# Attention feeding a maxout feed-forward layer on one Trainium2 core: the first batch's odd-token queries ahead of its even-token queries, with loads and transposes of the opening reordered

## The chip, the core and the metric

The kernel runs on one core of a Trainium2 chip. Its time is the device time of one execution in microseconds, as the median of several runs. Lower is better. The profile is that of one execution.

## The reference

The reference has two stages. Attention has 8 batches, 12 heads, 448 tokens and a head size of 64; its softmax adds exp(-max) to the denominator, so that the weights of a row may sum to less than one. The 3584 x 768 result goes through three 768 x 768 products, the largest of the three is kept for each element, and a fourth 768 x 768 product follows.

```python
def _attn_ref(q, k, v):
    scale = 1.0 / np.sqrt(q.shape[-1])
    scores = scale * np.matmul(q, k.transpose(0, 1, 3, 2))
    m = np.max(scores, axis=-1, keepdims=True)
    e = np.exp(scores - m)
    attn = e / (np.sum(e, axis=-1, keepdims=True) + np.exp(-m) + 1e-09)
    return np.matmul(attn, v).astype(np.float32)

def _moe_ref(x, w1, w2, w3, w_out):
    h = np.maximum(np.maximum(x @ w1, x @ w2), x @ w3)
    return (h @ w_out).astype(np.float32)
```

Since e / (sum e + exp(-m)) equals exp(s) / (sum exp(s) + 1) where s is the scaled score, the kernel takes exp(s) directly and needs no maximum.

## The kernel before

**Units of work.** The 12 heads of a batch are three groups of four heads, so there are 24 groups; group 0, 1 and 2 are batch 0, and group 3 begins batch 1. A group has two pairs of heads. One group's q, k and v are loaded by DMAs that GpSimd (POOL in the profile) issues in program order, with a cast from 32 to 16 bits: `load_qk` (L101, DMA at L113) and `load_v` (L118, two DMAs). `load_weight` (L133, L137) loads one of the four weights in three DMAs of two 128-row blocks each. Each of `ld_q`, `ld_k`, `ld_v` has four buffers, so group 4 uses the buffers of group 0.

**Attention of a group.** q and k must be transposed. `transpose_pe` (L182) transposes one pair's k and q blocks on TensorE into a PSUM tile `trT`, and copies them out into `KT` and `QT` with `evac`, on ScalarE (ACT) or VectorE (DVE). `transpose_once` (L217) transposes all of q or k, and then `shift_q` (L241) makes the shifted copy on POOL. `scores` (L285) multiplies 64-row blocks of k by the queries into PSUM tiles `stp`, and one exponential on ACT (L319) writes them to the buffer `e`. `av_tail` and `av_main` (L329, L348) multiply the exponentials by v, and DVE divides (L366 to L372) into `xn`. `prep_v` (L379) first copies v into the layout that they read, on DVE or POOL. `x_transpose_pe` (L392) transposes the result into `xT`, the input of the feed-forward layer.

**Feed-forward pieces.** `up_piece` (L430) makes two of six 128-row blocks of one of the three products for a range of batch 0's tokens, as 12 matmuls with 256 or 192 columns, in the order of the weights: w0 for the three pairs of blocks, then w1, then w2. DVE keeps the running maximum in `hT`. `out_piece` makes the last product. Pieces stand in a list, and `fill(cols)` takes pieces from it for as long as a credit of columns lasts, so that TensorE's program order mixes attention and pieces.

**Even and odd tokens.** In batch 0 the queries of each group are done in two parts: "E" is 256 of the 448 queries, "O" the other 192, selected by `part_blocks`. An opening loop does six steps: E of groups 0, 1, 2, and then O of groups 0, 1, 2. The loop over groups 3 to 23 follows, in three visits for each group. Step n computes scores of its own part and the product with v for the part before it. The first piece is made in step 3, and a piece of 256 columns goes with each half of steps 4 and 5 and with visits 0 and 1 of group 3. Visit 0 of group 3 also transposes q of group 4.

**The order on each engine is the program's.** The kernel runs under a manual schedule, so what is written first goes first on its engine. The pool `ps_s` has three PSUM tiles for scores, products with v and some transposes; `ps_b` has two, for the other transposes and the pieces.

**POOL's order before the change**: q of group 0, k of group 0 in two halves, the identity, q and k of group 1, v of 0, q and k of 2, v of 1, v of 2; then w0, `prep_v(1)`, q and k of 3, `prep_v(2)`, w1, w2, v of 3, k and q of 4, `shift_q(3)`, v of 4, k and q of 5, w_out. `prep_v(0)` is done by DVE.

Of the kernel before, what the change touches and what calls it, by code (L numbers as in the profile page):

```python
# [14 lines left out]
ts = bass.ts  # L15
# [6 lines left out]
def kernel(  # L22
# [78 lines left out]
    def load_qk(i, names="kq", prs=(0, NP)):  # L101
        b, g = groups[i]
        tiles = raw.setdefault(i, {})
        for nm in names:
            if nm not in tiles:
                t = ld_bufs[nm][i % NL]
                if nm == "q" and i < NF:
                    nc.vector.memset(t[:, 0 : NP * T + 2 : NP * T + 1, :], 0.0)
                tiles[nm] = t
            src = {"q": q, "k": k}[nm][b].rearrange("h s d -> (h s) d")  # L110
            src = src.rearrange("(g r x t) d -> g x r (t d)", g=NG, r=NP, x=P)[g]
            p0, p1 = prs
            nc.gpsimd.dma_start(  # L113
                out=tiles[nm][:, 1 : NP * T + 1].rearrange("x (r t) d -> x r (t d)", r=NP)[:, p0:p1],
                in_=src[:, p0:p1],
            )
# [16 lines left out]
    def load_weight(i, gs=(0, 1, 2)):  # L133
        w = (moe_w1, moe_w2, moe_w3, moe_w_out)[i]
        src = w.rearrange("(g hf p) f -> g p hf f", g=3, hf=2)
        for g in gs:
            nc.gpsimd.dma_start(out=w_sb[i][:, 2 * g : 2 * g + 2, :], in_=src[g])  # L137
# [1 line left out]

    wz = cpool.tile([128, 512], MMDT, name="wz")  # L140
    nc.vector.memset(wz, 0.0)
    load_qk(0, "q")
    load_qk(0, "k", (0, 1))
    load_qk(0, "k", (1, 2))
    ident16 = cpool.tile([128, 128], MMDT, name="ident16")
    make_identity(nc, ident16)
    load_qk(1)
# [10 lines left out]
        nc.vector.memset(vt_buf[j][:, :, D : D + 2], 1.0 / LAMBDA)  # L158
    for j in range(NEB):
        nc.vector.memset(e_buf[j][:, NB * S : NB * S + HP], 0.0)  # L160

    def warm(n, cols=512):
        ps = ps_b.tile([128, 512], FP32, tag="b", name="warm")
        for _ in range(n):
            nc.tensor.matmul(  # L165
                out=ps[:, 0:cols], lhsT=wz[:, 0:128], rhs=wz[:, 0:cols], start=True, stop=True
            )
# [8 lines left out]
    def evac(eng, dst, src):  # L176
        if eng is nc.scalar:
            nc.scalar.activation(out=dst, in_=src, func=AF.Copy)  # L178
        else:
            eng.tensor_copy(out=dst, in_=src)  # L180

    def transpose_pe(i, pr, pool, k_eng, q_engs):  # L182

        if pool is ps_s:
            both = ps_s.tile([128, 2, 1024], MMDT, tag="s", name="trT")
            tps = [both[:, 0], both[:, 1]]
        else:
            tps = [ps_b.tile([128, 1024], MMDT, tag="b", name="trT") for _ in range(2)]
        kr, qr = raw[i]["k"], raw[i]["q"]
        def tr(n, j, src, t):  # L190
            nc.tensor.transpose(  # L191
                out=tps[n][:, ts(j, 128)],
                in_=src[:, t + 1 : t + 3, :].rearrange("x t d -> x (t d)"),
                identity=ident16,
            )

        kj = (0, 1, 2) if pr == 0 else (3, 4, 5, 6)
        qt = (-1, 1, 3, 5, 0, 2, 4, 6) if pr == 0 else (8, 10, 12, 7, 9, 11, 13)
        for j, b in enumerate(kj):
            tr(0, j, kr, 2 * b)  # L200
        for j, t in enumerate(qt):
            tr(1, j, qr, t)
# [3 lines left out]
        evac(  # L206
            k_eng,
            KT[i][:, kj[0] * 128 : (kj[-1] + 1) * 128],
            tps[0][:, 0 : len(kj) * 128],
        )  # L210
        q0 = pr * 1024
        n = -(-len(qt) // len(q_engs))
        for e, eng in enumerate(q_engs):
            a, b = e * n * 128, min((e + 1) * n, len(qt)) * 128
            evac(eng, QT[i][:, q0 + a : q0 + b], tps[1][:, a:b])

    def transpose_once(i, nm, eng):  # L217

# [291 lines left out]
    def fill(cols):  # L510
        credit[0] += cols
        while pieces and credit[0] > 0:
            f, a, w = pieces.pop(0)
            f(*a)
            credit[0] -= w
        if not pieces:
            credit[0] = min(credit[0], 0.0)
# [2 lines left out]
        return sum(w for _, _, w in pieces)  # L520


    DV, AC = nc.vector, nc.scalar
    warm(10)
    transpose_pe(0, 0, ps_s, DV, (AC, DV))
    warm(3)
    transpose_pe(0, 1, ps_b, DV, (DV,))
    load_weight(0)
    prep_v(1, nc.gpsimd)
    load_qk(3)  # L530
    prep_v(2, nc.gpsimd)
    load_weight(1)

    parts = [(part, g) for part in "EO" for g in range(NG)]
    PW = {"E": (0, 1), "O": (2, 3), "EO": (0, 1, 2, 3)}
    UPE = 2 * NDC * (NE + 6)

    def av(i, ej, pr, part):
        av_tail(i, ej, pr, PW[part])
        av_main(i, ej, pr, PW[part])  # L540

    for n, (part, g) in enumerate(parts):
        ej = n % NEB
        pp, pg = parts[n - 1] if n > 0 else (None, None)
        step = UPE if n > 3 else 0
        nxt = g + 1 if part == "E" and g < NG - 1 else None
        scores(g, ej, (0, 1), part)
        if n != 3:
            scores(g, ej, (2, 3), part)
        if n > 0:  # L550
            av(pg, 1 - ej, 0, pp)
        if n > 1 and n != 4:
            x_transpose_pe(parts[n - 2][1], parts[n - 2][0])
        if n == 3:
            av(pg, 1 - ej, 1, pp)
            scores(g, ej, (2, 3), part)
        if n == 4:
            transpose_once(3, "q", AC)
        fill(step)
        if nxt is not None and n > 0:  # L560
            transpose_pe(nxt, 0, ps_b, AC, (DV,))
        scores(g, ej, (4, 5), part)
        scores(g, ej, (6,), part)
        if n == 0:
            warm(4)
            transpose_pe(nxt, 0, ps_b, DV, (DV,))
            prep_v(0, DV)
        if n == 3:
            x_transpose_pe(pg, pp)
            add_up(0, 0, NE, [(i, f) for i in range(3) for f in (0, 2, 4)])  # L570
            fill(UPE)
        if nxt is not None:
            transpose_pe(nxt, 1, ps_b, DV, (AC, DV) if n == 0 else (DV,))
        if n > 0 and n != 3:
            av(pg, 1 - ej, 1, pp)
        if n == 4:
            transpose_once(3, "k", AC)
        fill(step)
        if n == 1:
            load_weight(2)  # L580
        if n == 2:
            load_v(3)
            load_qk(4)
        if n == 4:
            shift_q(3, nc.gpsimd)
            load_v(4)
            load_qk(5)
            load_weight(3)


    visits = ((0, 1), (2, 3), (4, 5, 6))
# [18 lines left out]
    for i in range(3, NI):  # L610
        ej, pj = (i + 1) % NEB, i % NEB
        first = i == 3
        if PE_QK <= i + 2 < NI:
            transpose_dma(i + 2)
        if first:
            load_v(i + 2)
        for vi, units in enumerate(visits):
            n = 3 * i + vi
            scores(i, ej, units)
            if i == 4 and vi == 0:  # L620
                prep_v(i, DV)
            if vi < 2:
                av(i - 1, pj, vi, "O" if first else "EO")
            if vi == 1 and i > 3 * PE_X:
                x_transpose_dma(i - 1)
            if n in adds:
                add_batch(adds[n])
            per = UPE if first and vi < 2 else share(n)
            if vi == 0 and first:
                x_transpose_pe(1, "O")  # L630
            if vi == 2 and first:
                x_transpose_pe(i - 1, "O")
                fill(per / 2)
                prep_v(i, DV)
                add_up(0, NE, NO, [(w, f) for w in range(3) for f in (0, 2, 4)])
                add_out(0)
                per = share(n)
            if vi == 2 and 3 < i <= 3 * PE_X:
                x_transpose_all(i - 1)
            if first and vi == 1:  # L640
                transpose_once(i + 1, "q", AC)
                fill(per)
# [54 lines left out]
```

## Time and profile before

| | |
|---|---|
| median of 6 runs | 344.98 us |
| lowest, highest | 343.57, 346.86 us |
| profiled execution, its own time | 346.86 us |
| span of its instructions | 345.1 us |
| mean granted TensorE clock | 0.994 |
| TensorE (PE) busy | 331.7 us, 96% |
| VectorE (DVE), ScalarE (ACT), GpSimd (POOL) busy | 187.4, 151.7, 147.3 us |
| bytes moved by DMA, mean rate | 46.20 MB, 134 GB/s |

The profiled execution is the slowest of the six, and its own time is 1.8 us longer than its span. In the profile's lines, the first number of a timeline row is the start in us from the start of the span, the second how long it took, then engine, source line, operation, tile written and tiles read, shape and count; in square brackets is the idle time of the engine ahead of it and what ended it. Rates count bytes as written in 16 bits. A row with several shapes or instructions covers them all from the first start to the last end.

### The profile page before, as it was taken

The numbers are of one execution on the slowest core, as the hardware profiler recorded it, in microseconds if no ns is written. First come the engines' busy times: TensorE is split into PE (matmuls) and PEld (weight loads), VectorE is DVE, ScalarE is ACT, GpSimd is POOL, SyncE is SP. The second block draws the span as 40 slices with busy tenths as digits, with TensorE's granted clock in tenths as the row PEclk, the third lists the DMA queues.
The fourth block names the chain that finished last, engine by engine and source line by source line (L and its number), as shares of the span: only waits on it lengthen the run. The fifth ranks groups of instructions, "written<-read, shape, count | busy, mean of one in ns | idle before, by whom it ended". The sixth has DMA issues, their size and how long they took to land.

```text
span 345.1 us, 9827 instructions
## 1 busy us (share of the span) xinstructions
PE 331.7 (96%) x4184; PEld 200.6 (58%) x4184; DVE 187.4 (54%) x407; ACT 151.7 (44%) x181; POOL 147.3 (43%) x262
## 2 busy tenths in 40 slices
PE   8889699999999999999999999999999999999993
PEld 4668478866556555556555655556556555555552
DVE  2655357555556556556556555555556556465552
ACT  2876456566454444443443443453544444200000
POOL 8685558594683364272566075173354000000000
PEclk9999899999999999999999999999999999999999
DMA  7999999789897997979997999979982440133015
GB/s 103 187 208 209 201 163 159 111 132 216 147 140 119 200 218 106 123 113 238 144 125 105 189 195 123 110 126 220 135 145 10 122 123 3 33 76 93 0 41 144
DMA packets 84797, 46.20 MB, mean 134 GB/s; under 512 B 53264, under 2 KB 81296, under 8 KB 84752
## 3 DMA queue, kind: packets, MB, share of 16 engines
q0 software_dynamic: 29392, 22.03, 48.5%
q1 hardware_dynamic: 55120, 23.37, 38.0%
q8 instruction: 33, 0.54, 0.6%
q10 hardware_dynamic: 240, 0.16, 0.2%
q14 instruction: 12, 0.10, 0.1%
HBM read 44.04 MB, written 11.01 MB: 160 GB/s over the span
## 4 chain that ended last, share of the span: by engine, by line
PE 89%; ACT 4%; DMA 3%; DVE 1%; issue 1%; ACTq 0%
PE p_i L439 46%; PE op_ps L463 16%; PE stp L299 11%; PE avp L356 10%; DMA ld_q<-in_q_dram 3%; ACT e L319 3%; PE avp L339 2%; PE warm L165 2%; ACT QT L178 1%; PE trT L191 1%; PE trT L224 1%; PE xtp L412 0%; DVE QT L180 0%; DVE xn L372 0%; DVE xT L405 0%
## 5 line engine op out<-in xcount | busy, mean ns | idle before, releaser
L319 ACT ACTIVATE e<-stp 128x896 f16<-128x896 f32 (+4 forms) x171 | 144.1, 904 | 136.3 <-PE stp L299 136.3
L439 PE MATMUL p_i<-xT,w 128*128 128x448 f16 (+2 forms) x972 | 174.7, 333 | 0.3
L439 PEld LDWEIGHTS <-w 128*128 128x128 f16 x972 | 90.5, 98 | 68.0 <-issue 5.0
L244 POOL COPY QT<-QT 64x384 f16<-64x384 f16 (+1 forms) x84 | 46.7, 556 | 101.6 <-DMA QT<-ld_q 82.1
L450 DVE TENSOR_TENSOR hT<-hT,p_i 128x448 f16<-128x448 f16 (+2 forms) x96 | 59.6, 621 | 48.6 <-PE p_i L439 48.5
L463 PE MATMUL op_ps<-w,hT 128*128 128x384 f16 (+2 forms) x342 | 58.3, 323 | 0.0
L299 PE MATMUL stp<-QT,KT 64*64 64x448 f16 (+2 forms) x756 | 47.6, 338 | 1.7 <-DVE xn L372 0.7
L463 PEld LDWEIGHTS <-hT 128*128 128x128 f16 x342 | 32.1, 98 | 22.9 <-issue 2.0
L356 PE MATMUL avp<-vx,e 128*128 128x65 f16 x1152 | 45.4, 193 | 0.0
L470 DVE TENSOR_SCALAR o_sb<-op_ps 128x384 f32<-128x384 f32 (+2 forms) x57 | 31.3, 550 | 23.7 <-PE op_ps L463 22.8
L448 DVE CAST hT<-p_i 128x448 f16<-128x448 f32 (+2 forms) x48 | 30.0, 624 | 24.3 <-PE p_i L439 24.2
L356 PEld LDWEIGHTS <-e 128*128 128x128 f16 x1152 | 38.8, 97 | 2.2
L372 DVE TENSOR_TENSOR xn<-avp,rb 128x512 f16<-128x512 f32 (+1 forms) x54 | 34.1, 632 | 2.1 <-DVE rb L369 0.2
L299 PEld LDWEIGHTS <-KT 64*64 64x64 f16 x756 | 15.6, 105 | 26.3 <-issue 21.8
L366 DVE TENSOR_SCALAR rb<-avp 128x8 f32<-128x8 f32 (+1 forms) x54 | 8.9, 166 | 39.5 <-PE avp L356 39.4
L382 POOL COPY vx<-ld_v 128x768 f16<-128x768 f16 x21 | 17.2, 819 | 6.3 <-issue 3.7
L339 PEld LDWEIGHTS <-e 64*64 64x64 f16 x768 | 14.7, 107 | 7.8 <-PE stp L299 0.7
L113 POOL DMA_DIRECT2D ld_q<-in_q_dram x24 | 17.7, 740 | 3.2 <-PE stp L299 1.2
L113 POOL DMA_DIRECT2D ld_k<-in_k_dram x25 | 17.9, 718 | 2.5 <-PE avp L356 1.5
L126 POOL DMA_DIRECT2D ld_v<-in_v_dram x24 | 15.2, 634 | 2.1 <-DMA ld_q<-in_q_dram 1.1
L339 PE MATMUL avp<-vt,e 64*64 64x65 f16 x768 | 15.4, 192 | 0.6 <-DVE xn L372 0.5
L123 POOL DMA_DIRECT2D ld_v<-in_v_dram x24 | 15.2, 633 | 1.1 <-DMA ld_k<-in_k_dram 0.6
(40 smaller groups left out, 91.2 us busy)
## 6 DMA issues: line engine op xcount, KB each, us to landing
out_dram<-o_sb SPq DMA_DIRECT2D x54, 192.0 KB, 3.7
ld_v<-in_v_dram POOLq DMA_DIRECT2D x48, 128.0 KB, 4.9
ld_q<-in_q_dram POOLq DMA_DIRECT2D x24, 224.0 KB, 7.1
ld_k<-in_k_dram POOLq DMA_DIRECT2D x23, 224.0 KB, 6.7
w<-in_moe_w_dram POOLq DMA_DIRECT2D x9, 384.0 KB, 9.2
w<-in_moe_w_out_dram POOLq DMA_DIRECT2D x3, 384.0 KB, 9.3
xT<-xn SPq DMA_TRANSPOSE x18, 4.6
QT<-ld_q SPq DMA_TRANSPOSE x17, 5.9
```

The source lines that it names most:

```text
L113: nc.gpsimd.dma_start(out=tiles[nm][:, 1 : NP * T + 1].rearrange("x (r t) d -> x r (t d)", r=NP)[:, p0:p1], in_=src[:, p0:p1],)
L244: eng.tensor_copy(out=t[d0 : d0 + HP, o * 128 : (o + n) * 128], in_=t[s0 : s0 + HP, a * 128 : (a + n) * 128],)
L299: nc.tensor.matmul(out=stp[half * HP : half * HP + HP, par, j * qn : (j + 1) * qn], lhsT=k_block(i, pr, h2, x[half]), rhs=q_cols(i, pr, h2 ...
L319: nc.scalar.activation(out=dst, in_=src, func=AF.Exp, scale=scale)
L339: nc.tensor.matmul(out=ps[half * HP : half * HP + HP, hh, j * D1 : (j + 1) * D1], lhsT=eF[hh * HP : hh * HP + HP, o : o + HP], rhs=vt[hh * ...
L356: nc.tensor.matmul(out=ps[:, hh, j * D1 : (j + 1) * D1], lhsT=eF[:, o : o + 128], rhs=vx[:, 2 * pr + hh, (x[0]), 0:D1], start=False, stop= ...
L372: nc.vector.tensor_tensor(out=xn[i][:, pr, ws[0] : ws[0] + nw].rearrange("p j h d -> p h j d"), in0=acc[:, :, :, 0:D], in1=rb[:, :, 0:nw]. ...
L439: nc.tensor.matmul(out=p_i[:, j * qn : (j + 1) * qn], lhsT=w_sb[i][:, dc, ts(fc, 128)], rhs=xT[b][:, dc, q0 : q0 + qn], start=(dc == 0), s ...
L448: nc.vector.tensor_copy(out=dst, in_=src)
L450: nc.vector.tensor_tensor(out=dst, in0=dst, in1=src, op=ALU.max)
L463: nc.tensor.matmul(out=op_ps[:, 0:w], lhsT=hT[bp][:, fc, ts(t, 128)], rhs=wout_sb[:, fc, c : c + w], start=(fc == 0), stop=(fc == NFC - 1),)
L470: nc.vector.tensor_scalar(out=o_sb[:, c : c + w], in0=op_ps[:, 0:w], scalar1=1.0 / LAMBDA, scalar2=None, op0=ALU.mult,)
```

## The change

It has five parts.

1. Batch 0's order is turned: O (192 queries) of groups 0, 1, 2 first, then E (256 queries). The pieces for the O tokens are made first, 192 columns wide, two of them in step 3; the E pieces come after them. `STEP` takes the place of `UPE` as the credit. Since E is no longer written first, the columns of `e` between the parts are set to zero by a memset for each buffer.
2. In steps 0 to 2, scores of units 0 and 1 (which need the first pair only) come ahead of the second pair's transposes; before, all transposes of a group came ahead of its scores, or in the step before.
3. `transpose_pe` gives each job (k, and each part of q) a PSUM tile of its own in place of one shared tile or of one for k and one for q.
4. Group 0's k and q are loaded as k and q of pair 0, then k and q of pair 1.
5. POOL's order after v of 2 becomes: `prep_v(0)` (moved here from DVE), two thirds of w0, `prep_v(1)`, the last third of w0, q and k of 3, `prep_v(2)`, w1, **k and q of 4, w2, v of 3**, `shift_q(3)`, v of 4, k and q of 5, w_out.

```diff
-    load_qk(0, "q")
-    load_qk(0, "k", (0, 1))
-    load_qk(0, "k", (1, 2))
+    load_qk(0, "kq", (0, 1))
+    load_qk(0, "kq", (1, 2))
...
         nc.vector.memset(e_buf[j][:, NB * S : NB * S + HP], 0.0)
+        blk = e_buf[j][:, 0 : NB * S].rearrange("p (n s) -> p n s", s=2 * S)
+        nc.vector.memset(blk[:, :, NO : NO + HP], 0.0)
...
     def transpose_pe(i, pr, pool, k_eng, q_engs):
-        if pool is ps_s:
-            both = ps_s.tile([128, 2, 1024], MMDT, tag="s", name="trT")
-            tps = [both[:, 0], both[:, 1]]
-        else:
-            tps = [ps_b.tile([128, 1024], MMDT, tag="b", name="trT") for _ in range(2)]
+        def tile_of():
+            if pool is ps_s:
+                return ps_s.tile([128, 2, 1024], MMDT, tag="s", name="trT")[:, 0]
+            return ps_b.tile([128, 1024], MMDT, tag="b", name="trT")
...
+        n = -(-len(qt) // len(q_engs))
+        jobs = [(k_eng, "k", kj[0], kr, [2 * b for b in kj])]
+        for e, eng in enumerate(q_engs):
+            jobs.append((eng, "q", pr * 8 + e * n, qr, qt[e * n : (e + 1) * n]))
+        tps = [tile_of() for _ in jobs]
...
-    warm(3)
-    transpose_pe(0, 1, ps_b, DV, (DV,))
-    load_weight(0)
-    prep_v(1, nc.gpsimd)
+    prep_v(0, PL)
+    load_weight(0, (0, 1))
+    prep_v(1, PL)
+    load_weight(0, (2,))
     load_qk(3)
-    prep_v(2, nc.gpsimd)
+    prep_v(2, PL)
     load_weight(1)
-    parts = [(part, g) for part in "EO" for g in range(NG)]
-    UPE = 2 * NDC * (NE + 6)
+    STEP = 2 * NDC * (NO + 6)
+    parts = [(part, g) for part in "OE" for g in range(NG)]
     for n, (part, g) in enumerate(parts):
         scores(g, ej, (0, 1), part)
+        if n < 3:
+            if n == 0:
+                warm(2)
+            transpose_pe(g, 1, ps_b, DV, (DV,))
             scores(g, ej, (2, 3), part)
+            if n > 0:
+                av(pg, 1 - ej, 0, pp)
+            if n == 1:
+                transpose_pe(2, 0, ps_b, AC, (DV,))
+            if n == 2:
+                x_transpose_pe(0, "O")
+            scores(g, ej, (4, 5), part)
+            scores(g, ej, (6,), part)
+            if n > 0:
+                av(pg, 1 - ej, 1, pp)
+            else:
+                warm(4)
+                transpose_pe(1, 0, ps_b, AC, (DV,))
+                load_qk(4)
+                load_weight(2)
+                load_v(3)
+        elif n == 3:
             av(pg, 1 - ej, 0, pp)
+            x_transpose_pe(1, "O")
             av(pg, 1 - ej, 1, pp)
             scores(g, ej, (2, 3), part)
+            x_transpose_pe(2, "O")
+            add_up(0, NE, NO, [(i, f) for i in range(3) for f in (0, 2, 4)])
+            fill(STEP)
+            scores(g, ej, (4, 5), part)
+            scores(g, ej, (6,), part)
+            fill(STEP)
+        else:
+            scores(g, ej, (2, 3), part)
+            av(pg, 1 - ej, 0, pp)
+            if n == 4:
+                transpose_once(3, "q", AC)
+            else:
+                x_transpose_pe(0, "E")
+            fill(STEP)
+            scores(g, ej, (4, 5), part)
+            scores(g, ej, (6,), part)
             av(pg, 1 - ej, 1, pp)
+            if n == 4:
+                transpose_once(3, "k", AC)
+            fill(STEP)
+            if n == 4:
+                shift_q(3, PL)
+                load_v(4)
+                load_qk(5)
+                load_weight(3)
...
-                av(i - 1, pj, vi, "O" if first else "EO")
+                av(i - 1, pj, vi, "E" if first else "EO")
...
             if vi == 2 and first:
-                x_transpose_pe(i - 1, "O")
+                x_transpose_pe(i - 1, "E")
                 fill(per / 2)
                 prep_v(i, DV)
-                add_up(0, NE, NO, [(w, f) for w in range(3) for f in (0, 2, 4)])
+                add_up(0, 0, NE, [(w, f) for w in range(3) for f in (0, 2, 4)])
                 add_out(0)
```

Before, the loads of w2 stood at the end of step 1, and those of v of 3 and q and k of 4 at the end of step 2.

More of the change, by code (lines that the diff above doesn't have):

```diff
@@ L182, in transpose_pe @@
     def transpose_pe(i, pr, pool, k_eng, q_engs):
-        if pool is ps_s:
-            both = ps_s.tile([128, 2, 1024], MMDT, tag="s", name="trT")
-            tps = [both[:, 0], both[:, 1]]
-        else:
-            tps = [ps_b.tile([128, 1024], MMDT, tag="b", name="trT") for _ in range(2)]
-        kr, qr = raw[i]["k"], raw[i]["q"]
[L190 to L195, printed above, removed]
+        def tile_of():
+            if pool is ps_s:
+                return ps_s.tile([128, 2, 1024], MMDT, tag="s", name="trT")[:, 0]
+            return ps_b.tile([128, 1024], MMDT, tag="b", name="trT")
+        kr, qr = raw[i]["k"], raw[i]["q"]
         kj = (0, 1, 2) if pr == 0 else (3, 4, 5, 6)
         qt = (-1, 1, 3, 5, 0, 2, 4, 6) if pr == 0 else (8, 10, 12, 7, 9, 11, 13)
[L199 to L202, printed above, removed]
+        n = -(-len(qt) // len(q_engs))
+        jobs = [(k_eng, "k", kj[0], kr, [2 * b for b in kj])]
+        for e, eng in enumerate(q_engs):
+            jobs.append((eng, "q", pr * 8 + e * n, qr, qt[e * n : (e + 1) * n]))
         if i not in KT:
@@ L205, in transpose_pe @@
             QT[i] = att_pool.tile([P, (NB + 1) * 128], MMDT, tag="QT", name="QT")
[L206 to L215, printed above, removed]
+        tps = [tile_of() for _ in jobs]
+        for tp, (eng, nm, o, src, toks) in zip(tps, jobs):
+            for j, t in enumerate(toks):
+                nc.tensor.transpose(
+                    out=tp[:, ts(j, 128)],
+                    in_=src[:, t + 1 : t + 3, :].rearrange("x t d -> x (t d)"),
+                    identity=ident16,
+                )
+        for tp, (eng, nm, o, src, toks) in zip(tps, jobs):
+            dst = {"k": KT, "q": QT}[nm][i]
+            evac(eng, dst[:, o * 128 : (o + len(toks)) * 128], tp[:, 0 : len(toks) * 128])
     def transpose_once(i, nm, eng):
@@ L520, in left @@
         return sum(w for _, _, w in pieces)
-    DV, AC = nc.vector, nc.scalar
-    warm(10)
-    transpose_pe(0, 0, ps_s, DV, (AC, DV))
-    warm(3)
-    transpose_pe(0, 1, ps_b, DV, (DV,))
-    load_weight(0)
-    prep_v(1, nc.gpsimd)
-    load_qk(3)
-    prep_v(2, nc.gpsimd)
-    load_weight(1)
-    parts = [(part, g) for part in "EO" for g in range(NG)]
+    DV, AC, PL = nc.vector, nc.scalar, nc.gpsimd
     PW = {"E": (0, 1), "O": (2, 3), "EO": (0, 1, 2, 3)}
-    UPE = 2 * NDC * (NE + 6)
+    STEP = 2 * NDC * (NO + 6)
     def av(i, ej, pr, part):
@@ L540, in av @@
         av_main(i, ej, pr, PW[part])
+    warm(10)
+    transpose_pe(0, 0, ps_s, DV, (AC, DV))
+    prep_v(0, PL)
+    load_weight(0, (0, 1))
+    prep_v(1, PL)
+    load_weight(0, (2,))
+    load_qk(3)
+    prep_v(2, PL)
+    load_weight(1)
+    parts = [(part, g) for part in "OE" for g in range(NG)]
     for n, (part, g) in enumerate(parts):
@@ L544 @@
         pp, pg = parts[n - 1] if n > 0 else (None, None)
-        step = UPE if n > 3 else 0
-        nxt = g + 1 if part == "E" and g < NG - 1 else None
         scores(g, ej, (0, 1), part)
-        if n != 3:
+        if n < 3:
+            if n == 0:
+                warm(2)
+            transpose_pe(g, 1, ps_b, DV, (DV,))
             scores(g, ej, (2, 3), part)
-        if n > 0:
+            if n > 0:
[15 more added lines that the diff above has]
+        elif n == 3:
@@ L551 @@
             av(pg, 1 - ej, 0, pp)
-        if n > 1 and n != 4:
-            x_transpose_pe(parts[n - 2][1], parts[n - 2][0])
-        if n == 3:
+            x_transpose_pe(1, "O")
             av(pg, 1 - ej, 1, pp)
             scores(g, ej, (2, 3), part)
[L557 to L574, printed above, removed]
-            av(pg, 1 - ej, 1, pp)
-        if n == 4:
-            transpose_once(3, "k", AC)
@@ L578 @@
[L578 to L588, printed above, removed]
+            x_transpose_pe(2, "O")
[14 more added lines that the diff above has]
+            scores(g, ej, (6,), part)
+            av(pg, 1 - ej, 1, pp)
+            if n == 4:
[6 more added lines that the diff above has]
+                load_weight(3)
@@ L627 @@
                 add_batch(adds[n])
-            per = UPE if first and vi < 2 else share(n)
+            per = STEP if first and vi < 2 else share(n)
             if vi == 0 and first:
-                x_transpose_pe(1, "O")
+                x_transpose_pe(1, "E")
             if vi == 2 and first:
-                x_transpose_pe(i - 1, "O")
+                x_transpose_pe(i - 1, "E")
                 fill(per / 2)
                 prep_v(i, DV)
-                add_up(0, NE, NO, [(w, f) for w in range(3) for f in (0, 2, 4)])
+                add_up(0, 0, NE, [(w, f) for w in range(3) for f in (0, 2, 4)])
                 add_out(0)
```

## The prediction

> **What bounds the kernel now.** I read the engine shares first, then PE's waits in two stretches, then the order of time around the one long wait, then the loads behind it.
>
> ```profile
> PE 331.7 (96%) x4184; PEld 200.6 (58%) x4184; DVE 187.4 (54%) x407; ACT 151.7 (44%) x181; POOL 147.3 (43%) x262
> ```
>
> PE is the engine to look at. Its waits up to 44 us, and then from 44 us to the end:
>
> ```profile
> PE trT L224 <- DMA ld_q<-in_q_dram: 3.1, 1, 3.1
> PE warm L165 <- DVE wz L141: 1.2, 1, 1.2
> PE stp L299 <- DVE xn L372: 0.7, 1, 0.7
> PE avp L339 <- DVE xn L372: 0.5, 1, 0.5
> ```
>
> ```profile
> PE trT L224 <- ACT QT L178: 0.3, 1, 0.3
> ```
>
> After 44 us PE waits 0.3 us in 300. So whatever PE gains ahead of that point reaches the end one for one, and the opening decides. PE's order of time there:
>
> ```profile
> 36.35 0.57 PE L299 MATMUL stp<-QT,KT 64*64 64x448 f16 x8
> ...
> 37.31 0.38 PE L399 MATMUL xtp<-ident,xn 128*128 128x128 f16 x4
> 40.85 0.93 PE L224 MATMUL trT<-ident,ld_q 128*128 128x128 f16 x7 [3.15 <-DMA ld_q<-in_q_dram]
> 41.57 2.62 PE L439 MATMUL p_i<-xT,w 128*128 128x256 f16 x12
> 44.12 0.57 PE L299 MATMUL stp<-QT,KT 64*64 64x448 f16 x8
> ```
>
> In visit 0 of group 3, PE stops at 37.69 for q of group 4. When it goes on, a piece of 12 matmuls takes 2.62 us where others take 1.40 (from one start to the next, 27.58 to 28.98). The stretches of the wait, behind it and after that show why (columns: PE, PEld, DVE, ACT, POOL busy, then granted clock, DMA share, GB/s):
>
> ```profile
> 37.70:40.40 2.70, 0.00 (x0) 0.00 (x0) 0.87 (x3) 0.88 (x2) 2.20 (x4) 1.00 1.34 198
> 40.50:43.90 3.40, 3.05 (x18) 2.34 (x19) 0.00 (x0) 0.92 (x1) 1.51 (x3) 0.50 1.23 206
> 43.90:47.00 3.10, 3.04 (x50) 2.33 (x48) 1.48 (x5) 2.39 (x3) 0.00 (x0) 1.00 1.16 212
> ```
>
> The clock was halved for 3.4 us behind the gap: 7 transposes and a piece took 3.27 us (40.85 to 44.12), not 0.39 + 1.40 = 1.79. So the wait cost 3.15 + 1.5 us. The DMA engines were full meanwhile (198 GB/s), so the load was late by its place in the queue. POOL's order:
>
> ```profile
> 19.79 4.19 POOL L137 DMA_DIRECT2D w<-in_moe_w_dram  x6
> 24.58 0.62 POOL L123 DMA_DIRECT2D ld_v<-in_v_dram  x1 [0.60 <-DMA ld_k<-in_k_dram]
> 25.40 0.61 POOL L126 DMA_DIRECT2D ld_v<-in_v_dram  x1 [0.20 <-issue]
> 27.53 0.70 POOL L113 DMA_DIRECT2D ld_k<-in_k_dram  x1 [1.51 <-PE avp L356]
> 29.43 0.70 POOL L113 DMA_DIRECT2D ld_q<-in_q_dram  x1 [1.20 <-PE stp L299]
> ```
>
> The tile's own answers give the times to landing: 10.3 us for w1's last DMA (issued 21.2, landed 31.5), 13.9 us for w2's last (23.2, 37.2), 11.4 us for q of group 4 (29.4, 40.8). One after another at one rate: w2's three DMAs of 384 KB take 31.5 to 37.2, 1.9 us each or 202 KB/us; v of 3, k and q of 4 (704 KB) take 3.6 us. Both waits of POOL at the two loads end as an older DMA lands (w1's first two land at 27.0 and 28.9), whatever engine the brackets name.
>
> **Part 1: the order of loads.** k and q of 4 (448 KB) go ahead of w2 and v of 3. At 202 KB/us that is 2.2 us: q of 4 lands at 31.5 + 2.2 = 33.7 instead of 40.8, and the last of w2 at 37.2 + 2.2 = 39.4. v of 3 then lands where q did, at 40.8; its user, `prep_v(3)`, ran at 50.7. What is late next is w2: with two O pieces in step 3, the first w2 piece moves from visit 1 of group 3 to visit 0, just where the wait was.
>
> **Part 2: when PE gets there.** The steps laid end to end from rows of the trace:
> - The warming matmuls end at 5.64 as now. Group 0's transposes follow; with tiles of their own the copies overlap (now KT 6.76, QT 7.16, QT 7.79, each after the other), so scores start near 7.1 (now 8.26).
> - Exponentials of an O group take 0.75 three times and 0.43, together 2.7 us (rows 26.70, 29.39); those of an E group 3.35. Three O groups leave ACT 2 us less to do by step 3. These are moved, not saved.
> - The loads hold the front back: step 1 needs q of 1 (landed 10.7) and starts its scores near 12.4 (now 13.0); step 2 needs q of 2 (14.3) and starts near 16.7 (now 17.4). `prep_v(0)` on POOL waits for v of 0 (landed 12.0) and takes 0.82 + 0.29 + 0.29 = 1.4 us, done at 13.45, before its user at 14.4.
> - `prep_v(2)` now ends near 20.45 (0.6 later than now), behind w0's third part and two loads; the product with v of group 2 needs it near 21.3. Cover 0.8 us; without it, what it lacks is added.
> - In step 3 two products with v, DVE's 0.8 us after the last, and the transpose of it (the chain that now causes the 0.7 us wait) lead to the first piece near 24.2, its last third held for `xT` until 24.7. Now: 24.65 and 25.3. Gain here 0.5 us; bounds -0.5 and +1.5, since it is the sum of many short waits.
>
> From there PE is full: rest of the first piece, scores 0.45, piece 1.16 (24 matmuls of 192 columns from 53.10 to 55.42 are 2.32), then step 4 with scores 0.5 and 0.45, two products with v of 0.55, two transposes of 0.39, piece 1.16. It reaches the first w1 piece at 31.15. w1 lands at 31.5, and the first 4 of 12 matmuls (0.39) need only its first two DMAs, so there is no wait. Then three pieces (3.48), step 5 (scores, product, transpose 1.23, scores and product 0.92) and visit 0 (0.41 + 0.55 + 0.38 + 0.39) sum to 7.36: the w2 piece at 38.5. Four matmuls to 38.9, idle to 39.45, eight matmuls of 0.097, and scores of visit 1 at 40.3. They were at 44.12: **3.8 us earlier.** If PE is up to 0.5 us late at the first piece, the w2 wait absorbs it.
>
> **Part 3: what is left then.** Now three E pieces and nine O pieces remain at that point, 3 x 1.40 + 9 x 1.16 = 14.64. Afterwards two O and nine E remain, 14.92: **0.28 us lost**, since matmuls of 192 columns cost 0.097 us where their columns would give 0.08.
>
> **Part 4: loads delayed.** w0 is issued behind `prep_v(0)`, at 13.45 and not 11.6. It took 7.2 us to land; the shortest such time in the trace is 3.6 us for 224 KB, which with 160 KB more is 4.4. So 5.3 us are left where 4.4 are needed, and the cover is 0.9 us. The last third of w0, behind `prep_v(1)`, is issued near 17, two DMAs of 1.9 us ahead of it in the queue from 15. With four halves in front of the identity, k of 1 is issued 0.4 us later. I take a gap of 0.2 us in the stream (0 to 0.9): **0.2 us lost**. Splitting q of 0 in two is nothing: the three first loads landed 0.6 us apart, and the transposes wait for the warming matmuls anyway. [...]
>
> **Part 5: the rest.** Two memsets of 128x448 on DVE (nearest row 0.27 us) lie in its idle 5.2 us before 6.76; uncovered they would cost 0.6. One warming matmul fewer is 0.2 us within a wait for q of 1. `shift_q(3)` keeps its place, near 30 on POOL, for a user at 36.5.
>
> **Sum.** 3.8 - 0.28 - 0.2 = 3.3 us: 346.86 in the profiled execution becomes 343.6. The median, 344.98, is 1.9 us below that execution, and 1.5 us of the gain is the halved clock, which the one trace shows but not for the other runs. With it gain 3.3, without it 1.8; I take the middle, 2.6: **342.4 us**.
>
> [...]
>
> **Rivals.**
> - *The wait only changes its name* (17%). The stream slips by the whole 0.9 us, w2 lands at 40.3, and the runs of before lost no clock: 3.5 - 1.5 - 0.9 = 1.1, 343.9 us. For it: the DMA engines are full all through, and w2 is only 1.4 us sooner than q of 4 was. Against: v of 3 really moves out of the way.
> - *The early load doesn't help* (5%): POOL's semaphores or the queue let k and q of 4 land no earlier than 38, time 344.9. Against: their buffers are free from 9 us on, and loads landed in the order of issue.
> - *The front becomes a chain and slower than now* (10%). In steps 0 to 2 scores of units 2 and 3 now stand on PE behind transposes whose copies (0.42 + 0.61 on DVE) they need, and with two `ps_b` tiles a k copy on ACT (0.51) behind exponentials holds the next transpose. Uncovered, 1.6 us a step, 4.8 in three. The first piece then starts at 29.0. It decides from 26.7 (24.2, plus 0.5 of the w2 wait, plus 2.0); 4.8 - 0.5 - 2.0 is 2.3 us slower, 347.3. For it: DVE is busy 3.64 of 5 us at 15 to 20. Against: q of 1 and 2 and ACT's exponentials set the pace there, and copies lie under them.
>
> **How the numbers follow.** The forecast has 68%, its own range 341.0 to 343.2 (gain 3.3 + 0.7 for a median's scatter, to 1.8). Reaching to the first two rivals gives 341.0 to 345.0 and leaves out the chain and a little at the low end. This kernel's measurement tells 0.5%, 1.7 us, from no change: faster 0.68, same 0.17 + 0.05 = 0.22, slower 0.10.
>
> **What would show it.** Right: PE's 3.15 us wait for `ld_q` is gone; at most 1 us for `w` in visit 0 of group 3, near 39; clock 1.00 from 7 to 340; w2's last DMA lands near 39.4, q of 4 near 33.7; first piece near 24.2, scores of visit 1 near 40.3. Wrong: a first piece after 26, a wait for `w` over 1.5 us or with a halved clock behind it, w0 landing after 23.5, or PE idle again after 44 us.

## The result, and the profile after

The changed kernel's median is 344.76 us over 35 runs against 345.48 for the kernel before over 72: a ratio of 0.9986, 95% interval 0.9972 to 1.0. Ratios here and below leave out the few slow executions, over 1.5% above the fastest of the same kernel; medians count all. The forecast was 342.4. The absolute time lies in the range of the prediction, but the gain of 2.6 us that was forecast is not there: 0.7 us by the medians, 0.5 us by the ratio (interval 0 to 1.0). The profiled execution took 344.86 us with a span of 342.9; before, 346.86 and 345.1.

PE's waits after, first up to 44 us, then from 44 us to the end (who waited <- for what: us in total, times, longest):

```profile
PE stp L295 <- DVE QT L181: 1.8, 5, 0.8
PE warm L166 <- DVE wz L141: 1.2, 1, 1.2
PE trT L204 <- DMA ld_q<-in_q_dram: 1.2, 1, 1.2
PE p_i L435 <- DVE xT L401: 0.6, 1, 0.6
PE xtp L395 <- DVE xn L368: 0.4, 1, 0.4
```

```profile
PE trT L220 <- ACT QT L179: 0.6, 1, 0.6
```

The wait of 3.1 us for q of group 4 is gone. In its place stand 1.8 us for copies of QT (five times), 1.2 us for q of group 0, and 0.6 us twice for tiles in visits 0 and 1 of group 3. PE's order of time:

```profile
5.35 0.55 PE L204 MATMUL trT<-ident,ld_q 128*128 128x128 f16 x7
7.07 0.23 PE L204 MATMUL trT<-ident,ld_q 128*128 128x128 f16 x1 [1.17 <-DMA ld_q<-in_q_dram]
...
25.84 1.43 PE L435 MATMUL p_i<-xT,w 128*128 128x192 f16 x12
...
39.38 0.55 PE L220 MATMUL trT<-ident,ld_q 128*128 128x128 f16 x7
40.57 1.32 PE L435 MATMUL p_i<-xT,w 128*128 128x192 f16 x12 [0.64 <-DVE xT L401]
41.82 0.57 PE L295 MATMUL stp<-QT,KT 64*64 64x448 f16 x8
```

The eighth q transpose of pair 0 waits for a load that the other seven don't need. The first piece starts at 25.84 (24.65 before), and scores of visit 1 at 41.82 (44.12 before). In this execution the clock was halved in the opening (0.50 from 8.32 to 11.73 us) instead of behind 40 us (0.50 from 40.49 to 43.90 before); and the loads ran slower there. Stretches of the changed kernel (columns as before; the last three numbers are granted clock, DMA share and GB/s):

```profile
4.90:8.30 3.40, 1.92 (x22) 1.10 (x21) 0.78 (x2) 0.69 (x2) 3.40 (x6) 1.00 1.04 134
8.40:11.70 3.30, 3.04 (x34) 1.94 (x33) 1.05 (x2) 1.06 (x2) 1.71 (x4) 0.50 1.18 156
```

```profile
2.00:7.00 5.00, 3.90 (x19) 1.71 (x17) 0.41 (x2) 0.62 (x2) 4.92 (x10) 1.00 0.92 116
...
22.00:27.00 5.00, 4.34 (x95) 3.31 (x96) 3.14 (x13) 3.04 (x4) 3.60 (x6) 1.00 1.16 182
```

Before, the same two stretches moved 136 and 209 GB/s. By the tile's own answers the last DMA of w1 lands at 33.1 (31.5 before) and the last of w2, issued at 27.8, takes 13.2 us and lands at 41.0, where the prediction had 39.4.

The halving at 8.4 us is not what takes the gain. Halving the clock for 3.4 us takes 0.5% off the mean clock of an execution; 29 of the 36 executions of the changed kernel have a mean of 0.996 or more, so they lack it, and their median of 344.7 us is that of the other seven (344.9).

### The profile page after: what moved, and what is told of

It is laid out like the page before. It is cut to its first block, busy times and chain, and to the rows that moved or that the text cites. A ratio compares the mean times of both kernels' runs of the same rounds, so it can differ in the third digit from the quotient of the medians.

```text
span 342.9 us, 9832 instructions
## 1 busy us (share of the span) xinstructions
PE 331.5 (97%) x4183; PEld 200.3 (58%) x4183; DVE 187.2 (55%) x405; ACT 151.9 (44%) x181; POOL 148.9 (43%) x266
## 4 chain that ended last, share of the span: by engine, by line
PE 88%; DMA 5%; POOL 4%; issue 1%; ACT 1%; DVE 0%; POOLq 0%; ACTq 0%
PE p_i L435 47%; PE op_ps L459 16%; PE avp L352 11%; PE stp L295 11%; DMA w<-in_moe_w_dram 3%; DMA ld_v<-in_v_dram 2%; PE avp L335 2%; POOL ld_q L113 1%; POOL ld_k L113 1%; PE trT L220 1%; PE xtp L408 0%; POOL vx L378 0%; POOL w L137 0%; POOL ld_v L123 0%; ACT e L315 0%
## 5 line engine op out<-in xcount | busy, mean ns | idle before, releaser
L295 PE MATMUL stp<-QT,KT 64*64 64x448 f16 (+2 forms) x756 | 49.0, 341 | 2.0 <-DVE QT L181 1.8
L459 PEld LDWEIGHTS <-hT 128*128 128x128 f16 x342 | 32.1, 98 | 22.7 <-issue 2.0
L352 PEld LDWEIGHTS <-e 128*128 128x128 f16 x1152 | 38.8, 97 | 2.3
L362 DVE TENSOR_SCALAR rb<-avp 128x8 f32<-128x8 f32 (+1 forms) x54 | 8.9, 166 | 40.5 <-PE avp L352 40.3
L378 POOL COPY vx<-ld_v 128x768 f16<-128x768 f16 x22 | 18.0, 818 | 5.4 <-issue 2.9
```

Of the source, the lines that this page charges most:

```text
L295: nc.tensor.matmul(out=stp[half * HP : half * HP + HP, par, j * qn : (j + 1) * qn], lhsT=k_block(i, pr, h2, x[half]), rhs=q_cols(i, pr, h2 ...
L352: nc.tensor.matmul(out=ps[:, hh, j * D1 : (j + 1) * D1], lhsT=eF[:, o : o + 128], rhs=vx[:, 2 * pr + hh, (x[0]), 0:D1], start=False, stop= ...
L459: nc.tensor.matmul(out=op_ps[:, 0:w], lhsT=hT[bp][:, fc, ts(t, 128)], rhs=wout_sb[:, fc, c : c + w], start=(fc == 0), stop=(fc == NFC - 1),)
```

## Experiments

Two theories stood after the result. **A**: the early load is worth what was predicted, and the rest of the change gives it back, through the stream of loads and PE's own front. **B**: the wait of the kernel before costs little in a typical run, and its profile caught a bad one. Each kernel was timed beside runs of the kernel before. Ratios below are to those; the median of before was 345.6, 345.9 and 345.6 us in the three sets.

**1. The early load alone, on the kernel before.**

```diff
         if n == 1:
+            load_qk(4)
             load_weight(2)
         if n == 2:
             load_v(3)
-            load_qk(4)
```

> The kernel before with nothing changed but the place of the loads of k and q of group 4: ahead of w2 and v of 3. Theory A (the stream of loads: the early load itself is worth what was predicted, and the rest of the change gives it back): q of 4 lands near 34, the wait of 3.1 us at 37.7 is gone, no matmul of visit 0 of group 3 is late, since that visit still needs only w1, and w2 (landing near 39.4) is needed only near 40. Scores of visit 1 near 39.5 instead of 44.1: 3.1 us less than before without clock loss in the runs of before, 4.6 with it. Theory B (a typical run of before hardly pays for that wait, the profile caught a bad one): at most 1 us less than before.

Measured: 342.17 us, ratio 0.9894 (0.9868 to 0.992). Two moved loads make the kernel 1.1% faster; the whole change around them makes it 0.1% faster. PE in visits 0 and 1:

```profile
37.47 0.55 PE L224 MATMUL trT<-ident,ld_q 128*128 128x128 f16 x7
38.60 1.47 PE L439 MATMUL p_i<-xT,w 128*128 128x256 f16 x12 [0.58 <-DVE xT L405]
40.00 0.57 PE L299 MATMUL stp<-QT,KT 64*64 64x448 f16 x8
```

The load wait is gone, and visit 0's piece still needs w1 alone. A wait of 0.58 us comes to light that nobody expected: `ps_b` has two tiles, the transposes of xn take one and those of q the other, and the piece waits until DVE has copied the first into `xT`. Before, the load wait lay over it. Scores of visit 1 start at 40.0, 0.5 us later than expected for that reason. Theory B is out.

**2. The changed kernel with the late load.** k and q of 4 go back behind w2 and v of 3.

> The changed kernel with k and q of 4 put back behind w2 and v of 3. Theory A: q of 4 lands near 42.5, since the stream runs some 1.7 us later than in the kernel before; PE waits some 3 us for it in visit 0 of group 3 and the clock is halved behind it: 2 to 3 us slower than the changed kernel, 1.5 to 2.5 slower than before. Theory B: within 1 us of before and of the changed kernel.

Measured: 348.36 us, ratio 1.0069 (1.0045 to 1.0093), so by the ratios 2.4 us slower than before and 2.9 us slower than the changed kernel. The trace is that of an execution of 353.34 us, in which PE stopped for another 2.3 us near 230 us; only its opening is read here.

```profile
38.94 0.38 PE L395 MATMUL xtp<-ident,xn 128*128 128x128 f16 x4
42.17 0.92 PE L220 MATMUL trT<-ident,ld_q 128*128 128x128 f16 x7 [2.85 <-DMA ld_q<-in_q_dram]
```

PE goes on at 42.17, in the kernel before at 40.85. Without its early load the change makes the kernel slower.

**3 to 5. Which part gives it back.** Three kernels undo the new loads and copies of the opening, one by one and together:

```diff
# q of 0 whole (run 5)
-    load_qk(0, "kq", (0, 1))
-    load_qk(0, "kq", (1, 2))
+    load_qk(0, "q")
+    load_qk(0, "k", (0, 1))
+    load_qk(0, "k", (1, 2))
# v of 0 on DVE (run 3); both together in run 4
-    prep_v(0, PL)
-    load_weight(0, (0, 1))
+    load_weight(0)
     prep_v(1, PL)
-    load_weight(0, (2,))
...
                 transpose_pe(1, 0, ps_b, AC, (DV,))
+                prep_v(0, DV)
```

> The changed kernel with POOL's order of before for w0 (undivided, ahead of the copies of v) and the copy of v of group 0 back on DVE; the early load of group 4 kept. Theory A: w0 is issued near 11.9 and the weights land some 1.2 us sooner (last of w2 near 39.8 and not 41.0), but PE's first piece near 25.8 stays, so PE arrives at w2 at 40.5 as now: 0.3 to 0.8 us less than the changed kernel. Theory B: no difference from it.

> As the run with the copy of v of 0 on DVE, and group 0's q loaded whole and first, as in the kernel before, since the last transpose of pair 0's q reads the first token of pair 1. Theory A: PE's wait of 1.2 us for q of 0 near 6 is gone, the first piece starts near 24.7, the last of w2 lands near 39.4, and scores of visit 1 start near 40.4 to 40.8: 1.0 to 1.5 us less than the changed kernel, some 2 less than before. Theory B: no difference from the changed kernel.

> The changed kernel with one thing undone: q of group 0 is loaded whole and first, as before. It tells which of two late things sets the end. Theory A1 (the weights do: with the copies of v on POOL ahead of w0 they land 1.6 us later than summed, w2 near 41): PE gets to its first piece near 24.6 and not 25.8, no halved clock near 8, but waits more for w1 and w2; scores of visit 1 start near 41.3 to 41.8 as now, and the time is within 0.5 us of the changed kernel's. Theory A2 (PE's own front does): scores of visit 1 near 40.4, 1.2 us less than the changed kernel, as much as the run that also took the copy of v off POOL.

| | median us | ratio to before (95%) | last of w2 lands | scores of visit 1 |
|---|---|---|---|---|
| changed kernel | 344.76 | 0.9986 (0.9972 to 1.0) | 41.0 | 41.8 |
| v of 0 on DVE | 344.16 | 0.9972 (0.9942 to 1.0002) | 40.3 | 41.1 |
| both | 343.47 | 0.9933 (0.9909 to 0.9958) | 38.6 | 39.7 |
| q of 0 whole alone | 343.07 | 0.9926 (0.9893 to 0.9959) | 38.8 | 39.6 |

The weights come last, as theory A1 has it: in the first, second and last row, scores of visit 1 start 0.8 us after the last of w2 has landed, which are the eight matmuls of 0.097 us that need it. PE is close behind: the piece of 12 takes 1.08 us from its start to the next (38.62 to 39.70 in run 4), so from 40.57 in the changed kernel it would have ended 0.2 us sooner without that wait. But A1's cause, the copies of v on POOL, falls: with q of 0 whole, the weights land in time although these copies stand ahead of w0. The halves do it: undoing them alone brings PE's first piece from 25.84 to 23.96, w2 and visit 1 forward by 2.2 us, and the time by 2.1 us (by the ratios). Run 5 is still 1.1 us above the early load alone (0.9926 against 0.9894), but these intervals overlap. POOL's order in the changed kernel, then in the kernel with q of 0 whole, and w0's first two DMAs in the kernel with v of 0 on DVE (run 3):

```profile
11.61 0.61 POOL L126 DMA_DIRECT2D ld_v<-in_v_dram  x1 [1.59 <-DMA ld_q<-in_q_dram]
12.87 0.82 POOL L378 COPY vx<-ld_v 128x768 f16<-128x768 f16 x1 [0.65 <-DMA ld_v<-in_v_dram]
...
14.21 1.41 POOL L137 DMA_DIRECT2D w<-in_moe_w_dram  x2
```

```profile
10.17 0.61 POOL L126 DMA_DIRECT2D ld_v<-in_v_dram  x1 [0.46 <-DMA ld_q<-in_q_dram]
11.39 0.82 POOL L379 COPY vx<-ld_v 128x768 f16<-128x768 f16 x1 [0.60 <-DMA ld_v<-in_v_dram]
...
12.73 1.41 POOL L137 DMA_DIRECT2D w<-in_moe_w_dram  x2
```

```profile
12.22 1.44 POOL L137 DMA_DIRECT2D w<-in_moe_w_dram  x2
```

With the halves, q of 1 and v of 0 land later, POOL's copy starts 1.5 us later, and w0's first two DMAs are issued at 14.21 instead of 12.73. That later issue is not what makes the weights late: run 3, also with halves, issues them at 12.22, and w0's last DMA lands at 24.3, in the changed kernel at 24.1. The stream is late before w0. Where q of 0 is whole, it moves 135 and 208 GB/s in the stretches where the changed kernel had 116 and 182; of these, only the first goes with the halves, since run 3 has 115 and 208:

```profile
2.00:7.00 5.00, 3.97 (x20) 1.73 (x19) 0.79 (x3) 0.62 (x2) 4.92 (x10) 1.00 0.96 135
...
22.00:27.00 5.00, 4.45 (x75) 3.22 (x76) 2.58 (x10) 2.61 (x4) 3.46 (x5) 1.00 1.20 208
```

**6 and 7. Four halves on the kernel before**, in the changed kernel's order (k and q of pair 0, k and q of pair 1), and with both halves of q first. Nothing else is changed.

> The kernel before with the changed kernel's first loads alone (k and q of pair 0, then k and q of pair 1). Theory A2 (these halves are what spoils the opening: pair 0's last q transpose reads the first token of pair 1, and the stream of loads falls behind): PE waits some 0.5 to 1.3 us for q of 0 near 6, the weights land 0.8 to 1.5 us later than in before, so does q of 4 (near 42), and the time is 0.8 to 2 us above before. Theory E (in the kernel before the late q of 4 hides the front, and the stream is no slower by itself): within 0.5 us of before.

> The kernel before with four halves as well, but both of q first, then both of k. If the number of loads ahead of the identity makes the stream late, the last of w0 lands near 23.5 to 24.3 as with the other halves and the time is 0.5 to 1.5 us above before; if the place of q's second half does, it lands near 22.6 and the time is that of before within 0.5 us.

Measured: 346.23 us, ratio 1.0019 (0.9991 to 1.0047); and 345.69 us, ratio 0.9993 (0.9966 to 1.002). Neither time is told apart from before. In the two traces the stream moves 114 and 106 GB/s from 2 to 7 us (136 before), w0's last DMA lands at 23.3 and 24.0 (22.5 before), PE waits 0.7 us for q, or 0.9 us for k, of 0, and its first piece starts at 25.3 and 25.2. One trace is little to read a landing from: in the nine kernels with three first loads w0's last DMA lands between 22.1 and 23.8, in the five with four between 23.3 and 24.5 (medians 22.7 and 24.1). The rates from 2 to 7 us are 129 to 136 GB/s in the nine and 106 to 116 in the five. So the stream is late with four first loads, wherever q's second half stands; why a fourth load ahead of the identity costs that much was not found. On this kernel the run with the changed kernel's halves settles neither theory: its interval reaches from 0.3 us below before to 1.6 above. By the traces q of 4 lands 0.4 to 0.6 us later, and that is all that can reach the end, since its wait hides the rest of the front. Where the early load has uncovered the front, the halves cost more: by the ratios 1.3 us (run 3 against run 4, whose intervals overlap a little) and 2.1 us (the changed kernel against run 5, whose intervals do not).

**8. The order of even and odd.** The kernel of run 4 (both loads as before) with even-token queries first again; the edit swaps "O" and "E", `NO` and `NE` in the loops.

> The run with v of 0 on DVE and q of 0 whole, with the even-token queries first again (256-column pieces early, 192-column pieces late): the changed kernel without the turned order and without the two late loads. If the turned order costs (theory A: 0.8 us between visit 1 and the first quarter of the span, 84.15 us against 83.34 from the third exponential of group 3 to the 57th of its kind), this is 0.5 to 0.8 us faster than that run, near 342.7, with the wait for w2 at visit 0 a little later. Theory C (the rest of the changed front costs it: transposes between scores): no faster than that run.

Measured: 342.86 us, ratio 0.9916 (0.9888 to 0.9943), 0.6 us below run 4. That is what theory A expected, but the intervals overlap, so theory C is not excluded. The traces don't settle it: the last matmul ends at 335.9 in this kernel, at 336.3 in run 4 and at 335.7 in run 5, which has the turned order too. Whether the turned order itself costs some half a microsecond stays open.

**9 and 10. The second transposes.** Visits 0 and 1 of group 3 both transpose q of 4; the second does again what the first did. One condition takes the first away, on the kernel before and on that with the early load.

```diff
-            elif i + 1 < PE_QK and vi < 2:
+            elif i + 1 < PE_QK and vi < 2 and not first:
```

> The kernel before without the transposes of q of group 4 in visit 0 of group 3; visit 1 makes them anyway, so nothing is left out of the result. Theory A (the place on PE at which q of 4 is needed decides): PE goes on at 37.7 with the piece, scores of visit 1 start near 39.1, and it meets the same late load near 40.2 with some 0.6 to 0.8 us of wait and no halved clock. 3 to 4 us less than before, without any load moved. Theory D (it is DMA traffic as such that holds the opening back): at most 1 us less.

> The kernel before with the early load of group 4 and without the second transposes of its q. No wait in visits 0 and 1; against the early load alone it saves the 0.39 us of transposes and PE's wait of 0.6 us for a PSUM tile that DVE's copy into xT holds: 0.8 to 1.0 us less, near 341.2. If w2, landing at 38.8, came too late for visit 1, it would be less than 0.5.

Measured: 341.42 us, ratio 0.9882 (0.985 to 0.9915), with no load moved; and 341.08 us, ratio 0.9872 (0.9837 to 0.9907), with the early load. First the kernel without, then the one with it:

```profile
37.41 1.47 PE L439 MATMUL p_i<-xT,w 128*128 128x256 f16 x12
38.81 0.57 PE L299 MATMUL stp<-QT,KT 64*64 64x448 f16 x8
...
40.99 0.56 PE L224 MATMUL trT<-ident,ld_q 128*128 128x128 f16 x7 [1.07 <-DMA ld_q<-in_q_dram]
```

```profile
37.20 1.47 PE L439 MATMUL p_i<-xT,w 128*128 128x256 f16 x12
38.61 0.57 PE L299 MATMUL stp<-QT,KT 64*64 64x448 f16 x8
...
39.56 0.55 PE L224 MATMUL trT<-ident,ld_q 128*128 128x128 f16 x7
```

The same late load now meets a PE that has 2.5 us of other work (37.41 to 39.92), and what is left of the wait, 1.07 us, has no halved clock behind it: the seven transposes take 0.56 us, where they took 0.93 at 0.50 in the kernel before. Against the early load alone, the piece finds a free tile, and the time is 0.8 us (by the ratios) to 1.1 us (by the medians) lower, as expected, though with intervals that overlap. The last kernel has the lowest median of all that ran, 1.3% below before; from the kernel with no load moved, 0.3 us above it, it is not told apart.

**11 and 12. Two combinations.** The changed kernel with q of 0 whole and without the second transposes; and the fastest kernel with the change's PSUM tiles for each transposed part.

> The changed kernel with q of 0 whole and without the second transposes of q of group 4 in visit 0 of group 3. It saves 0.39 us of transposes and the 0.6 us wait for the tile that DVE's copy into xT holds, unless w2 (last DMA near 38.8) is too late for the piece of visit 0, which would then start near 37.5 and wait from 37.9 to 38.8. 0.3 to 1.0 us less than with q of 0 whole alone, 342.1 to 342.8; still above the 341.1 of the kernel before with the early load and without the second transposes, whose visit 0 needs only w1.

> The kernel before with the early load, without the second transposes, and with the changed kernel's PSUM tiles for each transposed part. The copies of group 0 overlap, scores start near 7.2 and not 8.2, but q of 1 (landed near 10) and the exponentials set the pace from step 1 on: at most 0.5 us less than without the tiles, and no difference if the loads alone set it.

Measured: 343.61 us, ratio 0.9915 (0.989 to 0.9939); and 341.75 us, ratio 0.987 (0.9847 to 0.9894). Neither gains. The first shows what the change has made of visit 0:

```profile
37.50 0.56 PE L436 MATMUL p_i<-xT,w 128*128 128x192 f16 x4
39.49 0.83 PE L436 MATMUL p_i<-xT,w 128*128 128x192 f16 x8 [1.43 <-DMA w<-in_moe_w_dram]
```

With two pieces in step 3, visit 0 needs w2, and PE waits 1.43 us for its last DMA: all that the condition saves goes into that wait, and scores of visit 1 start at 40.3 (39.6 in run 5). The tiles bring scores of group 0 forward by 0.1 us alone (7.91, and 7.99 without them; 7.2 was expected), and the first piece starts at 24.9, where it started at 24.3 without them.

## Why the prediction was wrong

**Right:** the bound, the place and the worth of moving the load. The wait for q of 4 is gone, PE's remaining waits behind 44 us are 0.6 us in all, and the loads of that order alone are worth 3.4 us by the medians, 3.7 by the ratio (prediction: 3.3 in the profiled execution for the whole change; it did not price the loads alone).

**Part 4, the term that failed: "Splitting q of 0 in two is nothing", and 0.2 us for a gap in the stream.** The delay was 1.6 us at w1 and w2, and w2 came last at visit 1. Run 5 undoes the split alone: w2 lands 2.2 us sooner and the kernel takes 2.1 us less. Its gain over before, 2.6 us by the ratio, is then the one that was forecast. That is in part luck: visit 1 is 4.5 us ahead of before there and not 3.8, and Part 3 costs more than its 0.28 us.

Two readings went wrong. The prediction held that pair 0's transposes wait for the warming matmuls anyway; but a q transpose takes two token columns, and the last of pair 0 takes one of pair 1, so it needs the second half, which now came last: 1.17 us of wait. With the weights landing as late as they did, that wait alone adds nothing, since visit 1 follows w2. And the stream's delay was bounded by w0's cover of 0.9 us, part by part, with the copy of v on POOL ahead of w0 as its main cause. The copy is not the cause: with q of 0 whole no cost of it shows (ratio 0.9926 with it, 0.9933 without), and with the halves w0's last DMA lands at 24.1 with it and at 24.3 without it. Between the changed kernel and run 3 the last of w1 and w2 land 0.8 us apart, but run 2 has the copy too and its w1 lands as in run 3 (32.3), so this is no more than one trace differs from another. Four first loads in place of three make the stream late from its start; the cause of that stays open.

**Part 2, the first piece at 24.2.** It was at 25.84, a loss of 1.2 us where the bounds of the gain were -0.5 and +1.5; part of it may be the halved clock of that execution, for run 3, which has the halves but no halved clock and v of 0 on DVE, has 24.76. With q of 0 whole it starts at 24.14, 23.96 and 23.83 (runs 4, 5 and 11), so the walk of the opening was right to 0.4 us for the loads that it assumed. The rival of the chain named a mechanism that is there, copies of QT that scores of units 2 and 3 wait for, but priced it at 4.8 us; it measures 1.8 to 2.0, in front of waits that had to be sat out anyway.

**The sum at visit 1, 3.8 us, was 2.3** in the two profiles (44.12 to 41.82), because both ends of the race were late: the last of w2 at 41.0 instead of 39.4, which came last, and PE at the w2 piece at 40.57 instead of 38.5. The 0.6 us for the `xT` copy was counted at nothing: in the profile of before the load wait lies over it. It is part of PE's 40.57, and it decides in run 4, where w2 lands at 38.6 and visit 1 starts 1.1 us later.

**Part 3, 0.28 us, was 0.8**: from visit 1 to the last matmul the changed kernel takes 296.1 us (41.82 to 337.9), the kernel before 295.3 (44.12 to 339.4). Both reach the scores of visit 2 after 3.56 us, the changed kernel with a smaller piece but a longer wait for a copy of QT (0.58 us, before 0.26); there 0.5 us more are columns still to do by the prediction's own prices (1.16 + 9 x 1.40 against 2 x 1.40 + 9 x 1.16); the rest was not traced. So 1.5 us are left of the sum at the last matmul of the two profiles. The medians show 0.7, for the profiled execution of before was 1.4 us above its median. The 0.08 us that the prediction set for 192 columns is near what wider matmuls give in the trace of before: 18 of 448 columns take 3.50 us (160.84 to 164.34), 0.194 each, which is 0.083 for 192.

**The halved clock.** The prediction took the middle between runs with and without its 1.5 us. The runs tell: of 63 runs of the kernel before, 16 have a mean granted clock of 0.996 or more, which leaves no room for such a halving; they all took 344.61 us or less, with a median of 344.1. The other 47 all took 345.03 us or more, with a median of 345.9. So most runs do pay. The two traces show the halving in different places: before, at 40.49 us, 2.8 us after PE had stopped at 37.69; in the changed kernel at 8.32 us, after a stretch in which PE was busy 1.92 of 3.40 us. Against the 16 runs that don't pay, the changed kernel gains nothing.

**The rival nearest to the result** is "the wait only changes its name", at 17%: it forecast a gain of 1.1 us, and 0.7 was measured. In its mechanism, a stream that is late where the wait was, it is right; its number is near by luck. It took 0.9 us for the slip, where 1.6 was measured, and runs of before that lose no clock, where 47 of 63 do.

## What to carry to other kernels

Where a DMA stream holds the kernel back, the position in it of the transfer that is needed first is worth trying by itself, ahead of any rearrangement around it: here two moved loads gave 1.1%, and the rearrangement took most of it back. A long wait in a profile lies over the waits of everything beside it (tiles, copies, later loads), so a sum that removes it has to price each of those again. Before a load is split, list which elements each consumer reads, the last one too; and before a load is moved, ask whether its first consumer has to stand where it stands, since leaving out one repeated transpose was worth as much. And before one trace's landing is put down to one edit, see how far the same landing moves between traces that share the edit: w0's last DMA moved by up to 1.7 us between the nine traces with three first loads.

## What the hardware showed that was not expected

In these traces the clock's halving does not follow from the length of one gap. It came behind a gap of 2.85 us (run 2; PE busy 0.55 us from 38.8 to 42.2, then the clock at 0.50 to 45.6: seven transposes took 0.92 us and a piece 2.13, at 46.21 and 46.60 they took 0.55 and 1.15), and after a stretch of 3.4 us with PE busy 56% (1.92 of 3.40 us, the changed kernel), and did not come where a gap of 3.05 us fell over two stretches with PE busy 1.76 and 1.99 of 3.40 us (the kernel before with four halves, run 6):

```profile
36.60:40.00 3.40, 1.76 (x37) 1.17 (x34) 1.76 (x6) 1.73 (x2) 2.15 (x4) 1.00 1.33 199
40.00:43.40 3.40, 1.99 (x23) 1.63 (x27) 0.08 (x1) 0.92 (x1) 2.10 (x4) 1.00 1.29 202
43.40:46.00 2.60, 2.60 (x47) 2.19 (x40) 1.37 (x4) 2.29 (x3) 0.00 (x0) 1.00 1.17 213
```

In the traces of the kernel before, of the changed kernel and of run 6, the changes of the granted clock lie whole multiples of 3.413 us apart (before: 6.36, 40.49, 43.90 and 344.27; changed: 4.90, 8.32, 11.73 and 342.82; run 6: 5.90 and 340.41), and the stretches of 3.40 us are laid by that spacing. A wait of 3.15 us cost the kernel before 1.5 us more behind it (seven transposes and a piece in 3.27 us), one of 3.05 us cost run 6 its length alone (the same in 1.80 us, 41.41 to 43.21). What decides between the two was not shown: the stretch with 1.92 us of PE's work had the halving behind it, the one with 1.76 had none.

In the traces of the kernel before and of the changed kernel POOL never had more than eight DMAs under way (of 109 and 110), and they landed in the order of issue. With eight under way, the next was issued only when the oldest had landed: in the kernel before, k of group 4 at 27.53 behind the first of w1 at 27.00, and q at 29.43 behind the second at 28.90. And one load cut in two at the head of the stream cost 13 to 30 GB/s of 129 to 136 from 2 to 7 us, and 1.4 us at the landing of the first weight (by the medians of five and nine traces); the cause stays open.
